# A state-space layer and a SwiGLU block on one NeuronCore: another order for the steps of a hand-scheduled kernel

## The chip, the core and the metric

The kernel runs on one core of a Trainium2 chip. A core has five engines with a queue of instructions each: TensorE (PE: matrix products and transposes, into PSUM), VectorE (DVE), ScalarE (ACT), GpSimd (POOL) and SyncE (SP, which issues the transfers here). Each engine takes its own queue strictly in order; engines wait for one another through semaphores. The metric is the device time of one execution in microseconds, as the median of several.

## The reference

A Mamba-2 layer (4 batches, 8 heads, 768 positions, head width 32, state width 16, chunks of 32 positions), whose output becomes 3072 tokens of 256 features, followed by an RMS norm and a SwiGLU block:

```python
log_a = np.log(np.clip(a, 1e-06, 1.0))
for c in range(nc):
    cum = np.cumsum(la, axis=-1)
    L = np.exp(cum[:, :, :, None] - cum[:, :, None, :]) * causal
    CB = np.einsum('bhin,bhjn->bhij', Cc, Bc)
    y_intra = np.einsum('bhij,bhjd->bhid', CB * L, xc)
    y_inter = np.einsum('bhin,bhnd->bhid', Cc, state) * np.exp(cum)[:, :, :, None]
    y[:, :, sl] = y_intra + y_inter
    Bx = np.einsum('bhjn,bhjd->bhjnd', Bc, xc) * decay_from_j[:, :, :, None, None]
    state = decay_full[:, :, None, None] * state + np.sum(Bx, axis=2)
x = y.transpose(0, 2, 1, 3).reshape(B * S, H * D)          # 3072 x 256
xn = x / np.sqrt(np.mean(x * x, -1, keepdims=True) + 1e-06) * rms_g
g = xn @ w_gate                                            # 256 x 1536
silu = g * (1.0 / (1.0 + np.exp(-g)))
return (silu * (xn @ w_val) @ w_out).astype(np.float32)    # 1536 x 256
```

The weights come in as 64-bit floating-point words.

## The kernel before

The work is one function. The 3072 tokens are six blocks of 512; a block is two pairs, a pair two stretches of 128 positions. For each pair the state-space part runs: load B, C (`bc`) and x (`x`), transpose them on PE (`turn`, with the copies out of PSUM `T`, `Tt`, `Td`), build the decays (`mask` L443 and `sums` L457/L464 on PE, `exp` on ACT, or by rows through DRAM with `row`, `rowout`, `rowe`, `tok`, `spread`, `sub`, `ex`), products of C and B (`g` L572/L579), their multiplication by the decays on DVE (`L`, `L1`; L618, L612), states (`A` L644 on PE, `S` L658 to L668 on DVE) and outputs (`y`, L685 to L716). Then follow squares, transposes and norm of a block (`sq`, `yt`, `ms`, `rs`, `rb`, `xn`).

The SwiGLU block of the first two pairs of block 0 is done plainly (`early`, `norm`; `gate.2` to `gate.5` at L845, `silu`, `hid` L878). Everything after uses a scheme with seven products in place of eight: sums of the weights (`cw` L900) and of the activations (`tx` L908), products `P.k.j` (L931), a copy of one of them by ACT (`take` L937), a sum on DVE (`C` L943), `silu` on ACT and the multiplication of both halves (`hid`, L956). The second projection of block 0 is plain (`o`); the later blocks use a similar scheme of larger order (`two`, `u`, `O` L1052, totals `w` L1083), and `put` stores the result.

Weights are loaded in twenty pieces (`fetch.k`, L148 to L160: pieces 0 to 3 of 256 KB, the rest of 512 KB) and turned from 64-bit words into 32-bit numbers: three activations for the exponent (`pow.k`, L184 to L190), two DVE operations for the mantissa (`man.k`, L209 and L212), and one that multiplies them (`wt.k`, L218).

The order of all this is written out. Under `tc.manual_schedule()` nothing is rearranged: a string `order` of 1649 steps is read from left to right, and each step emits its instructions on the queues of the engines that it uses. A step reads `block:kind.numbers/slots*fillers`; slots are the PSUM pairs (0, 1, 2) that it takes, and `c*2` puts two warm-up products ahead of the step `c`. The `p` at the end of a kind (`cwp`, `txp`, `hidp`, `up`, `twop`, `subp`) puts the same elementwise operation on POOL instead of DVE. So moving a step in the string moves all of its instructions in their engines' queues, its transfers on SP's queue included. There are eight semaphores for transfers; each transfer waits for the landing of the one eight before it. The loop that reads the string:

```python
for step in order.split():
    step, _, slots = step.partition("/")
    blk, _, step = step.partition(":")
    ...
    if blk == "0":
        first_kinds[kind](*numbers)
    else:
        kinds[kind](int(blk), *numbers)
```

Of the kernel before, what the change touches and what calls it, by code (L numbers as in the profile page):

```python
# [20 lines left out]
def kernel(  # L21
# [35 lines left out]
    P = 128  # L57
# [6 lines left out]
    T = NB * S  # L64
# [1154 lines left out]
    def of_chunk(n, fn):  # L1219
# [32 lines left out]
        0:mask.0.0/0 0:whole 0:hmask 0:tmask 0:part 0:gcol 0:part2 1:exps 0:after2 0:mask.0.1/1  # L1252
        0:fetch.3 0:aT 0:sel 0:la0 0:turn.0.1 0:T.0.1 0:Tt.0.1.1 0:log4.4.2 0:mask.1.1/2 0:Tt.0.0.1
        0:fetch.4 0:log4.0.4 0:r.0 0:parts.0 0:log 0:d 0:dx 0:log4.6.2 0:turn.0.0 0:Tt.0.0.0
        0:Tt.0.1.0 0:sums.0.1 0:exp.0.1 0:fetch.2 0:middles 0:T.0.0 0:sums.1.1 0:scale.0 0:sums.0.0
        0:kinks 0:scale.1 0:bc.2 0:turn.1.1 0:exp.0.0 0:T.1.1 0:Tt.1.1.1 0:Tt.1.0.1 0:man.0 0:c*2
        0:fetch.5 0:man.1 0:g.0.1/1 0:L.0.1 0:cx 0:exp.1.1 0:g.0.0/0 0:never16 0:last.1 0:Tl.1
        0:turn.1.0 0:Tt.1.0.0 0:fetch.8 0:L.0.0 0:T.1.0 0:Tt.1.1.0 0:mask.1.0/1 0:pow.0 0:A.0
        0:fetch.11 0:cc 0:S.0 0:A.1 0:sums.1.0 0:S.1 0:g.1.0/2 0:exp.1.0 0:L.1.0 0:pow.3 0:g.1.1/0
        0:eps 0:row.1 0:last.0 0:Tl.0 0:y.0/1 0:rowout.1 0:rowe.1 0:L.1.1 0:scale.2 0:fetch.7 0:wt.0  # L1260
        0:y.1/2 0:fetch.6 0:sq.0 0:pow.1 0:r.1 0:dT.2 0:turn.2 0:yt.0 0:x.2 0:man.3 0:wt.1 0:sq.1
        0:yt.1 0:pow.2 0:bc.3 0:parts.1 0:wt.3 0:T.2 0:man.2 0:wt.2 0:mask.3/1 0:man.4 0:early.0.0/0
        0:mask.2/2 0:man.5 0:ms.0 0:x.3 0:pow.4 0:rs.0 0:xn.0 0:sums.3 0:txp.0.0 0:tx.0.2 0:sums.2
        0:row.0 0:exp.3 0:Tt.2.0 0:Tt.2.1 0:fetch.9 0:Td.2 0:rowe.0 0:early.0.1 0:norm.0 0:pow.5
        0:exp.2 0:early.1.0/1 0:wt.5 0:early.1.1 0:silu.0 0:rowout.0 0:wt.4 0:fetch.10 0:man.6
        0:man.7 0:pow.7 0:norm.1 0:A.2 0:S.2 0:hid.0 0:gate.2/0 0:bc.5 0:table.0 0:pow.6 0:wt.7
        0:man.9 0:wt.6 0:gg.2/1 0:L1.2.3 0:L.2.0 0:silu.2 0:scale.3 0:man.8 0:pow.8 0:pow.9 0:hid.2
        0:gate.3/2 0:L1.2.2 0:wt.8 0:silu.3 0:hid.3 0:wt.9 0:pow.10 0:man.10 0:gate.4/1 0:y.2/2
        0:fetch.15 0:man.11 0:silu.4 0:wt.10 0:table.1 0:ydone.1 0:pow.11 0:ydone.0 0:S.3 0:sq.2
        0:scale.5 0:hid.4 0:yt.2 0:cw.3.0 0:cwp.3.1 0:gate.5/0 0:silu.5 0:wt.11 0:hid.5 0:cw.3.3  # L1270
        0:dT.3 0:turn.3 0:T.3 0:Tt.3.0 0:fetch.13 0:switch.1 0:Tt.3.1 0:Td.3 0:pow.13 0:man.13
        0:P.2.3 0:switch.0 0:P.2.4 0:P.1.3 0:fetch.12 0:cw.4.0 1:table 0:gg.3/2 0:take.1.3 0:cwp.4.1
        0:P.1.4 0:take.1.4 0:tx.0.1 0:cwp.3.2 0:P.6.3 0:L1.3.2 0:take.6.3 0:L.3.0 0:tok 0:L1.3.3
        1:dT.1 0:silu.1 0:cwp.4.2 0:C.11.3 0:P.6.4 0:take.6.4 0:P.7.3 0:C.11.4 0:wt.13 0:P.5.3
        0:tokout 0:take.7.3 0:fetch.14 0:pow.12 0:x.4 0:P.7.4 0:txp.0.3 0:P.4.3 0:man.14
        0:silug.11.4 0:C.22.3 0:silug.22.3 0:hidgp.22.3 0:bc.4 0:scale.4 0:man.12 0:x.5 0:P.3.3
        0:wt.12 0:silug.21.3 0:y.3/2 0:hidg.21.3 0:pow.14 0:P.1.5 0:C.12.3 0:P.2.5 1:S.0 1:S.1
        0:spread.10 0:spread.8 0:fetch.19 0:take.7.4 0:take.1.5 0:cwp.5.0 0:fetch.16 0:cwp.5.1
        0:spread.11 0:sq.3 0:P.5.4 0:fetch.17 0:C.22.4 0:P.6.5 0:hidgp.11.4 0:yt.3 0:wt.14
        0:take.6.5 0:cw.5.2 0:silug.12.3 0:P.4.4 0:ms.1 0:hidgp.12.3 0:C.11.5 0:silug.21.4 0:rs.1  # L1280
        1:spread.0 0:hidg.21.4 0:man.15 0:exps 0:hid.1 0:o.0/2 0:P.7.5 0:cw.1.0 0:cwp.4.3 0:P.3.4
        0:cw.1.1 0:C.12.4 0:pow.15 0:wt.15 0:cw.1.2 1:turn.0 1:T.0 0:silug.11.3 0:hidg.11.3
        0:silug.11.5 0:silug.12.4 0:hidg.12.4 0:take.7.5 0:rb.1 0:pow.16 0:P.5.5 0:o.1 0:o.2
        0:C.22.5 0:silug.22.4 0:man.16 0:P.4.5 0:silug.22.5 0:cw.1.3 0:cwp.5.3 0:cw.0.0 0:hidgp.11.5
        0:P.3.5 0:C.12.5 0:fetch.18 1:turn.1 0:silug.12.5 1:T.1 1:Tt.1.1 0:xn.1 0:silug.21.5 0:o.3
        0:cwp.0.2 0:hidg.21.5 1:P.1.0 1:take.1.0 0:txp.1.0 0:txp.1.2 1:P.2.0 0:tx.1.1 1:P.1.1
        0:ydone.3 0:wt.16 0:cwp.0.1 0:hidgp.22.4 1:P.6.0 1:P.2.1 1:bc.1 1:C.11.0 0:man.17 1:Tt.1.0
        1:take.1.1 1:silu.11.0 1:P.6.1 1:take.6.1 1:cwp.2.0 0:o.4 1:C.11.1 1:P.5.1 0:hidgp.12.5
        1:hid.11.0 0:hidgp.22.5 0:man.19 1:take.6.0 0:pow.19 0:wt.19 1:silu.11.1 1:P.7.1 1:take.7.1
        0:subp.10 0:txp.1.3 1:P.5.0 1:P.7.0 0:spread.9 1:P.4.1 1:C.22.1 1:P.3.1 1:Tt.0.0 1:silu.22.1  # L1290
        1:spread.3 1:hidp.22.1 1:Td.1 1:take.7.0 1:C.22.0 1:silu.21.1 1:P.4.0 0:pow.17 0:cw.0.3
        1:P.3.0 1:hid.21.1 0:man.18 1:silu.21.0 1:hid.11.1 1:C.12.0 0:ydone.2 1:spread.2 1:hid.21.0
        1:sub.0 1:cwp.2.2 1:P.1.2 0:sub.8 1:take.1.2 0:o.5 0:wt.17 1:C.12.1 1:sub.3 1:silu.12.0
        0:pow.18 1:hid.12.0 0:wt.18 1:two.2 1:cwp.2.1 1:P.6.2 1:Tt.0.1 1:P.1.3 1:take.1.3 1:take.6.2
        1:P.2.2 1:two.3 0:sub.11 1:P.2.3 1:P.7.2 1:silu.22.0 0:o.6 1:P.6.3 1:hid.22.0 0:o.7 1:x.0
        1:take.7.2 1:C.11.2 1:C.11.3 1:cw.2.3 1:P.5.2 2:dT.0 1:scale2.1 1:two.11 1:sub.2 1:ex.0
        0:sub.9 1:two.0 1:silu.11.2 1:P.4.2 1:take.6.3 0:ex.9 0:ex.8 1:two.1 1:twop.4 1:silu.11.3
        1:C.22.2 1:hid.11.3 1:P.7.3 1:take.7.3 1:silu.22.2 1:P.5.3 1:P.3.2 1:C.12.2 1:twop.6
        1:silu.12.1 1:hid.12.1 1:ex.3 1:C.22.3 0:o.8 1:silu.21.2 1:hid.21.2 1:P.4.3 1:bc.0
        1:silu.21.3 1:hid.21.3 1:scale2.0 0:o.9 1:hid.22.2 1:P.3.3 1:C.12.3 1:two.9 1:P.1.5  # L1300
        1:silu.22.3 1:take.1.5 1:P.1.4 1:take.1.4 0:o.10 0:o.11 1:hid.22.3 1:P.2.5 1:silu.12.3
        1:hidp.12.3 1:P.2.4 1:hid.11.2 1:P.6.4 1:C.11.5 1:spread.1 0:ex.10 0:ex.11 1:ex.2 1:dT.0
        1:Td.0 1:C.11.4 1:P.6.5 1:silu.11.5 0:put.0 0:put.3 0:put.1 0:put.2 1:g 1:L1.3 1:silu.11.4
        1:take.6.4 1:take.6.5 1:L 1:twop.8 1:L1.2 1:P.7.4 1:P.7.5 1:hid.11.5 1:P.5.4 1:take.7.4
        1:take.7.5 1:P.4.4 1:P.4.5 1:silu.12.2 1:two.5 1:C.22.4 1:y.0 1:silu.22.4 1:hid.11.4
        1:hidp.12.2 1:silu.21.5 1:hid.21.5 1:u.1 2:S.0 1:P.5.5 1:hid.22.4 1:silu.21.4 1:hid.21.4
        1:u.0 1:two.7 1:C.22.5 1:P.3.4 1:O.2.0 1:silu.22.5 1:C.12.4 1:silu.12.4 1:O.2.1 1:hid.22.5
        1:O.15.0 1:O.15.1 1:w.0 1:w.2 2:bc.1 1:x.1 1:u.2 1:y.1 2:S.1 1:P.3.5 1:C.12.5 1:O.3.0
        1:subp.1 1:O.3.1 1:sq 2:spread.2 1:yt 1:silu.12.5 1:O.0.0 1:O.0.1 1:hidp.12.5 1:O.6.0 1:up.9
        2:turn.0 1:u.3 1:ms 1:w.4 1:O.17.0 1:u.4 1:O.17.1 1:rs 1:w.5 1:w.10 1:O.6.1 1:O.16.0  # L1310
        1:O.16.1 1:w.1 1:u.5 1:O.4.0 1:rb 1:O.4.1 1:O.9.0 2:T.0 2:turn.1 1:u.6 1:O.9.1 1:w.6
        1:hidp.12.4 1:up.7 1:w.3 1:u.10 1:u.11 1:O.8.0 1:O.8.1 1:O.13.0 1:O.18.0 1:O.18.1 1:w.11
        1:O.13.1 1:O.11.0 1:w.12 1:w.8 2:dT.1 1:up.12 1:O.11.1 1:O.12.0 1:O.12.1 1:w.13 1:w.16 1:xn
        1:txp.0 1:txp.1 1:O.5.0 1:O.5.1 2:Tt.0.1 2:Tt.0.0 1:w.7 1:w.9 1:u.8 1:w.20 1:two.10 2:P.1.1
        2:take.1.1 2:P.1.0 1:O.7.0 1:O.7.1 1:up.13 1:w.14 1:w.17 1:w.15 2:take.1.0 2:P.6.1 1:w.18
        1:tx.2 2:P.6.0 1:u.14 1:O.1.0 2:take.6.1 1:O.1.1 1:up.15 1:O.14.0 1:O.14.1 1:O.19.0
        2:spread.0 1:w.19 1:O.19.1 2:spread.3 1:w.22 2:Td.0 1:w.24 2:T.1 2:Tt.1.1 1:O.10.0 2:Tt.1.0
        1:w.23 2:take.6.0 1:O.10.1 1:w.25 1:w.21 2:P.7.1 2:P.2.1 2:C.11.1 2:P.2.0 1:ex.1 2:P.7.0
        2:P.5.1 2:silu.11.1 2:take.7.0 2:C.11.0 2:Td.1 2:g 1:tx.3 2:sub.3 2:take.7.1 2:scale2.1
        2:P.4.0 2:silu.21.0 2:C.22.1 2:hid.11.1 2:silu.11.0 2:hid.11.0 2:hid.21.0 2:P.5.0 2:C.22.0  # L1320
        2:P.4.1 2:silu.21.1 2:subp.0 2:P.3.1 2:silu.22.1 2:x.0 2:L1.2 2:P.1.2 2:bc.0 2:scale2.0
        2:hid.21.1 2:hidp.22.1 2:take.1.2 2:C.12.1 2:silu.12.1 2:hidp.12.1 2:P.3.0 2:L 2:P.1.3
        2:take.1.3 2:P.6.2 2:take.6.2 2:P.2.3 2:C.12.0 2:L1.3 2:subp.2 2:C.11.3 2:y.0 2:silu.12.0
# [132 lines left out]
```

## Time and profile before

| what | us |
|---|---|
| median of 3 runs | 397.82 (397.78, 397.82, 398.51) |
| the profiled execution | 399.72 |
| its span, first to last instruction | 398.0 |
| mean granted clock of TensorE | 0.991 |
| first product of the scheme, L931 | starts at 55.19 |
| `mask.1.0`, the second pair's decays | starts at 15.77 |
| `r.1`, after the second pair's outputs | starts at 25.00 |

The profile is of one execution. "Busy" counts the time in which an engine runs an instruction; PE's counts the modelled ends of pipelined matmuls, so that a busy PE may still be waiting between them. The granted clock is the share of full speed at which TensorE was allowed to run. A timeline line gives the start, the length, engine, line, operation, output and input tiles with their shapes, and in brackets the idle time before it with what ended it.

### The profile page before, as it was taken

Reading aid. Unit: us, or ns where it says so; the run is one execution under the profiler, and the core shown is the slowest. Engines: PE = TensorE matmul, PEld = TensorE weight load, DVE = VectorE, ACT = ScalarE, POOL = GpSimd, SP = SyncE. Lnnn points to the kernel's source line nnn. Section 1 sums busy time; section 2 is a strip of 40 time slices with the busy share of each in tenths; the row PEclk is TensorE's granted clock in tenths of the full one; section 3 lists DMA queues with packets and bytes.
Section 4 is the critical chain, followed back from the end, with each engine's and each line's share of the span. In section 5 each row is a group of like instructions: output and inputs, shape, how many; then the busy total and the mean of one; then the engine's idle time right before and its main releaser. Section 6 shows DMA issues by size and latency. Waiting matters only on the chain.

```text
span 398.0 us, 9646 instructions
## 1 busy us (share of the span) xinstructions
PE 388.4 (98%) x3841; PEld 333.8 (84%) x3841; DVE 285.0 (72%) x617; ACT 236.2 (59%) x492; POOL 136.0 (34%) x157
## 2 busy tenths in 40 slices
PE   8799999999999999999999999999999999999996
PEld 4566468888887889988899988899988899988995
DVE  7789999998955877676586565677563577465684
ACT  3689989968898372556774534486256541455420
POOL 3110024366094345422276512144712042210121
PEclk9789999999999999999999999999999999999999
DMA  9898988275000516205013310210100001100001
GB/s 111 191 302 151 234 153 237 60 167 99 2 1 14 94 37 138 74 2 94 29 48 79 71 25 2 41 43 21 41 2 2 0 2 33 54 1 2 1 2 53
DMA packets 92469, 27.01 MB, mean 68 GB/s; under 512 B 77416, under 2 KB 86248, under 8 KB 92424
## 3 DMA queue, kind: packets, MB, share of 16 engines
q1 hardware_dynamic: 88264, 26.13, 29.9%
q10 hardware_dynamic: 4160, 0.26, 0.8%
q8 instruction: 30, 0.49, 0.5%
q14 instruction: 15, 0.12, 0.1%
HBM read 22.64 MB, written 3.74 MB: 66 GB/s over the span
## 4 chain that ended last, share of the span: by engine, by line
PE 79%; ACT 9%; DVE 4%; DMA 3%; issue 2%; SPq 1%; DVEq 0%; ACTq 0%
PE gate L931 27%; PE o L1052 22%; PE val L931 20%; PE o L963 4%; ACT e L190 3%; PE y L716 2%; DMA xr<-in_x_dram 2%; PE g L579 1%; DMA wr<-in_moe_w_gate_dram 1%; ACT L184 1%; ACT sq L190 1%; SPq L128 1%; DMA br<-in_B_dram 1%; ACT L L190 1%; PE tp L522 1%
## 5 line engine op out<-in xcount | busy, mean ns | idle before, releaser
L943 DVE TENSOR_TENSOR c<-val,p 128x512 f32<-128x512 f32 x99 | 67.2, 686 | 46.4 <-PE val L931 35.1
L937 ACT COPY p<-gate 128x512 f32<-128x512 f32 x99 | 56.9, 584 | 58.4 <-PE gate L931 57.4
L931 PE MATMUL gate<-tx,wgv 128*128 128x256 f32 x264 | 65.3, 380 | 0.0
L956 POOL TENSOR_TENSOR hid<-c 128x256 f32<-128x256 f32 x36 | 28.9, 805 | 106.1 <-ACT c L190 104.1
L190 ACT ACTIVATE c<-c 128x256 f32<-128x256 f32 x99 | 39.4, 414 | 33.6 <-DVE c L943 33.2
L931 PEld LDWEIGHTS gate<-tx,wgv 128*128 128x128 f32 x264 | 49.7, 190 | 7.1 <-issue 0.3
L1083 DVE TENSOR_TENSOR ob<-ob,o 128x128 f32<-128x128 f32 (+1 forms) x90 | 23.9, 297 | 24.1 <-PE o L1052 18.4
L956 DVE TENSOR_TENSOR hid<-c 128x256 f32<-128x256 f32 x63 | 28.3, 457 | 17.5 <-ACT c L190 15.6
L1052 PE MATMUL o<-two,hid 128*128 128x128 f32 x280 | 36.6, 276 | 0.2 <-ACT ob L190 0.2
L1052 PEld LDWEIGHTS o<-two,hid 128*128 128x128 f32 x280 | 34.1, 192 | 1.1 <-ACT ob L190 0.4
L931 PE MATMUL gate<-xn,wgv 128*128 128x256 f32 x132 | 33.6, 383 | 0.4 <-DVE hid L956 0.4
L931 PE MATMUL val<-tx,sw 128*128 128x256 f32 x132 | 33.8, 380 | 0.0
L931 PE MATMUL gate<-tx,sw 128*128 128x256 f32 x132 | 33.4, 382 | 0.0
L931 PE MATMUL val<-xn,sw 128*128 128x256 f32 x132 | 33.4, 381 | 0.0
L931 PE MATMUL val<-xn,wgv 128*128 128x256 f32 x132 | 32.8, 381 | 0.4 <-DVE hid L878 0.4
L492 POOL TENSOR_SCALAR_AFFINE_SELECT L<-L 64x512 f32<-64x512 f32 x32 | 24.9, 779 | 18.0 <-ACT L L190 16.6
L931 PEld LDWEIGHTS val<-xn,wgv 128*128 128x128 f32 x132 | 24.8, 190 | 4.0 <-DVE hid L878 0.7
L190 ACT ACTIVATE e<-e,kinks 128x512 f32<-128x512 int16 (+3 forms) x40 | 27.2, 679 | 1.3
L931 PEld LDWEIGHTS gate<-xn,wgv 128*128 128x128 f32 x132 | 24.3, 190 | 4.3 <-DVE hid L956 0.8
L931 PEld LDWEIGHTS val<-tx,sw 128*128 128x128 f32 x132 | 24.9, 190 | 3.4
L931 PEld LDWEIGHTS val<-xn,sw 128*128 128x128 f32 x132 | 24.6, 190 | 3.4 <-issue 0.2
L931 PEld LDWEIGHTS gate<-tx,sw 128*128 128x128 f32 x132 | 24.3, 190 | 3.4 <-issue 0.2
(203 smaller groups left out, 720.0 us busy)
## 6 DMA issues: line engine op xcount, KB each, us to landing
L<-rowd SPq DMA_DIRECT2D x32, 128.0 KB, 3.1
xr<-in_x_dram SPq DMA_DIRECT2D x24, 128.0 KB, 3.6
wr<-in_moe_w_out_dram SPq DMA_DIRECT2D x6, 512.0 KB, 6.9
out_dram<-ob SPq DMA_DIRECT2D x24, 128.0 KB, 1.8
wr<-in_moe_w_gate_dram SPq DMA_DIRECT2D x5, 512.0 KB
wr<-in_moe_w_val_dram SPq DMA_DIRECT2D x5, 512.0 KB, 5.7
br<-in_B_dram SPq DMA_DIRECT2D x22, 64.0 KB, 3.8
cr<-in_C_dram SPq DMA_DIRECT2D x22, 64.0 KB, 4.2
```

Of the source, the lines that this page charges most:

```text
L128: queue.dma_start(out=st[p]["x"][:, i], in_=x[b, :, sl, :].rearrange("h s n -> s h n"))
L184: nc.scalar.preload_act_table_set("natural_log_exp_and_others")
L190: nc.scalar.activation(**operands)
L492: nc.gpsimd.affine_select(out=L[r], in_=L[r], pattern=[[0, NH], [1, HC]], compare_op=ALU.is_ge, fill=0.0, base=0, channel_multiplier=-1)
L716: nc.tensor.matmul(out=y[2 * k + u][rows, (2 * n + i) * HC:(2 * n + i + 1) * HC], start=(k, u, rows.start) not in opened, stop=True, skip_ ...
L931: nc.tensor.matmul(out=dst[:, half[w]], lhsT=lhsT, rhs=rhs, start=(k in (1, 2, 5) and w == 0), stop=True, skip_group_check=True)
L937: nc.scalar.copy(out=t, in_=Xs[j])
L943: nc.vector.tensor_tensor(out=t, in0=Zs[j], in1=a, op=ALU.add)
L956: engine.tensor_tensor(out=hid[:, 2 * j + c // 10 - 1, c % 10 - 1], in0=u, in1=src[:, half[1]], op=ALU.mult)
L963: nc.tensor.matmul(out=o, lhsT=hid[:, f, k // 2, (k % 2) * P:(k % 2 + 1) * P], rhs=wo[:, f], start=opens, stop=(f == NF - 1), skip_group_c ...
L1052: nc.tensor.matmul(out=Os[blk, b][:, place * P:(place + 1) * P], lhsT=hidden_or_sum(u)[:, g], rhs=rhs, start=(blk, b) not in opened, stop= ...
L1083: nc.vector.tensor_tensor(out=o, in0=o, in1=src, op=ALU.add if what[0] == "+" else ALU.subtract)
```

## The change

One string is replaced: `order`. Its first 25 steps and its last 3 are the same; the 1621 between stand in another order. The steps are the same but for some that change their engine between DVE and POOL (`cw` and `cwp`, `tx` and `txp`, `hid` and `hidp`, `u` and `up`, `two` and `twop`, `sub` and `subp`): DVE has 445 elementwise operations of two tensors instead of 459, POOL 123 instead of 109. 2016 matmuls, 299 activations, 26 table loads and 189 transfers stay.

Named by what comes first in each queue: `man.0`, `man.1` and `pow.0` stand behind both halves `L.0.1`, `L.0.0` instead of ahead of them; `aT` is ahead of `mask.0.1`; the two filler products come ahead of `turn.0.0`; `cc`, `A.0` and `S.0` come ahead of `g.0.1`; the weights' pieces are fetched in another order (11, for one, behind `rowout.0`, where it stood behind 8); `turn.2`, `turn.3` and `tok` come between the plain products of block 0 instead of behind them; the gates run 2, 3, 5, 4 instead of 2, 3, 4, 5. The beginning of both:

```diff
-        0:mask.0.0/0 0:whole 0:hmask 0:tmask 0:part 0:gcol 0:part2 1:exps 0:after2 0:mask.0.1/1
-        0:fetch.3 0:aT 0:sel 0:la0 0:turn.0.1 0:T.0.1 0:Tt.0.1.1 0:log4.4.2 0:mask.1.1/2 0:Tt.0.0.1
-        0:fetch.4 0:log4.0.4 0:r.0 0:parts.0 0:log 0:d 0:dx 0:log4.6.2 0:turn.0.0 0:Tt.0.0.0
-        0:Tt.0.1.0 0:sums.0.1 0:exp.0.1 0:fetch.2 0:middles 0:T.0.0 0:sums.1.1 0:scale.0 0:sums.0.0
-        0:kinks 0:scale.1 0:bc.2 0:turn.1.1 0:exp.0.0 0:T.1.1 0:Tt.1.1.1 0:Tt.1.0.1 0:man.0 0:c*2
-        0:fetch.5 0:man.1 0:g.0.1/1 0:L.0.1 0:cx 0:exp.1.1 0:g.0.0/0 0:never16 0:last.1 0:Tl.1
-        0:turn.1.0 0:Tt.1.0.0 0:fetch.8 0:L.0.0 0:T.1.0 0:Tt.1.1.0 0:mask.1.0/1 0:pow.0 0:A.0
-        0:fetch.11 0:cc 0:S.0 0:A.1 0:sums.1.0 0:S.1 0:g.1.0/2 0:exp.1.0 0:L.1.0 0:pow.3 0:g.1.1/0
-        0:eps 0:row.1 0:last.0 0:Tl.0 0:y.0/1 0:rowout.1 0:rowe.1 0:L.1.1 0:scale.2 0:fetch.7 0:wt.0
-        0:y.1/2 0:fetch.6 0:sq.0 0:pow.1 0:r.1 0:dT.2 0:turn.2 0:yt.0 0:x.2 0:man.3 0:wt.1 0:sq.1
...
+        0:mask.0.0/0 0:whole 0:never16 0:hmask 0:tmask 0:fetch.2 0:part 0:eps 0:fetch.4 0:aT
+        0:after2 0:part2 0:mask.0.1/1 0:turn.0.1 0:la0 0:log4.4.2 0:T.0.1 0:Tt.0.0.1 0:mask.1.1/2
+        0:log4.0.4 0:log4.6.2 0:Tt.0.1.1 0:r.0 0:kinks 0:parts.0 0:log 0:d 0:middles 0:c*2 0:sel
+        0:dx 0:turn.0.0 0:scale.0 0:Tt.0.1.0 0:cx 0:sums.0.1 0:exp.0.1 0:Tt.0.0.0 0:fetch.3 0:gcol
+        1:exps 0:bc.2 0:sums.1.1 0:T.0.0 0:fetch.5 0:sums.0.0 0:exp.0.0 0:scale.1 0:cc 0:turn.1.1
+        0:T.1.1 0:A.0 0:S.0 0:g.0.1/1 0:L.0.1 0:g.0.0/0 0:last.1 0:Tt.1.1.1 0:fetch.8 0:Tt.1.0.1
+        0:exp.1.1 0:Tl.1 0:turn.1.0 0:T.1.0 0:Tt.1.1.0 0:Tt.1.0.0 0:bc.3 0:L.0.0 0:fetch.7 0:man.0
+        0:pow.0 0:man.1 0:mask.1.0/1 0:sums.1.0 0:g.1.1/0 0:g.1.0/2 0:L.1.1 0:exp.1.0 0:L.1.0
+        0:last.0 0:Tl.0 0:A.1 0:y.0/1 0:S.1 0:y.1/2 0:pow.1 0:sq.0 0:yt.0 0:wt.0 0:r.1 0:man.2
+        0:row.1 0:pow.4 0:wt.1 0:rowout.1 0:parts.1 0:sq.1 0:fetch.6 0:pow.2 0:wt.2 0:early.0.0/0
...
```

The steps around the first products of the scheme, before:

```diff
-        0:fetch.15 0:man.11 0:silu.4 0:wt.10 0:table.1 0:ydone.1 0:pow.11 0:ydone.0 0:S.3 0:sq.2
-        0:scale.5 0:hid.4 0:yt.2 0:cw.3.0 0:cwp.3.1 0:gate.5/0 0:silu.5 0:wt.11 0:hid.5 0:cw.3.3
-        0:dT.3 0:turn.3 0:T.3 0:Tt.3.0 0:fetch.13 0:switch.1 0:Tt.3.1 0:Td.3 0:pow.13 0:man.13
-        0:P.2.3 0:switch.0 0:P.2.4 0:P.1.3 0:fetch.12 0:cw.4.0 1:table 0:gg.3/2 0:take.1.3 0:cwp.4.1
...
```

and after:

```diff
+        0:fetch.10 0:rowe.0 0:rowout.0 0:exp.2 0:xn.0 0:early.0.1 0:early.1.0/1 0:txp.0.0 0:norm.0
+        0:silu.0 0:turn.2 0:man.7 0:hid.0 0:man.6 0:tok 0:ydone.1 0:tokout 0:early.1.1 0:gate.2/0
+        0:norm.1 0:pow.6 0:fetch.11 0:T.2 0:Tt.2.1 0:Tt.2.0 0:txp.0.2 0:ydone.0 0:wt.6 0:cwp.1.0
+        0:dT.2 0:man.11 0:turn.3 0:txp.0.1 0:Td.2 0:gate.3/2 0:pow.7 0:wt.7 0:dT.3 0:T.3 0:Tt.3.0
+        0:x.2 0:Tt.3.1 0:Td.3 0:silu.2 0:hid.2 0:gg.2/1 0:man.8 0:cw.1.1 0:L1.2.3 0:L.2.0 0:pow.11
+        0:wt.11 0:fetch.9 0:silu.3 0:man.10 0:pow.8 0:L1.2.2 0:gate.5/0 0:hid.3 0:pow.10 0:x.3
+        0:wt.8 0:A.2 0:S.2 0:silu.5 0:hid.5 0:cwp.1.2 0:tx.0.3 0:pow.9 0:man.9 0:wt.9 0:cwp.3.0
+        0:table.1 0:gate.4/1 0:silu.4 0:hid.4 0:pow.13 0:wt.10 0:y.2/2 0:S.3 0:cwp.3.1 0:cw.3.3
+        0:yt.2 0:cw.0.0 0:cwp.3.2 0:switch.1 0:P.2.3 0:switch.0 0:P.1.3 0:take.1.3 0:C.11.3 0:P.2.4
...
```

## The prediction

> **What bounds the kernel now.** I read the busy totals first, then PE's waits, then windows by stage, then the timeline where the windows show a hole.
>
> ```profile
> PE 388.4 (98%) x3841; PEld 333.8 (84%) x3841; DVE 285.0 (72%) x617; ACT 236.2 (59%) x492; POOL 136.0 (34%) x157
> PE e L443 <- DVE L L618: 2.6, 1, 2.6
> PE val L931 <- DVE hid L878: 0.4, 1, 0.4
> PE o L1052 <- DVE ob L1083: 0.4, 1, 0.4
> ```
>
> PE is busy for 98% of the span, and one wait stands out: `mask.1.0` (L443) is held 2.6 us, with DVE's `L` (L618) named. The windows tell whether "busy" means "the bound". Columns: window, length, then busy time and count of PE, PEld, DVE, ACT, POOL, then granted clock, DMA share, GB/s.
>
> ```profile
> 16.00:17.00 1.00, 1.00 (x14) 0.28 (x16) 0.97 (x2) 0.00 (x0) 0.00 (x0) 0.50 0.38 53
> 21.00:22.00 1.00, 1.00 (x8) 0.67 (x7) 0.58 (x4) 0.32 (x1) 0.00 (x0) 0.50 1.00 383
> 25.00:55.00 30.00, 29.10 (x344) 17.09 (x340) 29.14 (x65) 28.63 (x50) 2.43 (x3) 1.00 0.91 207
> 55.20:394.00 338.80, 337.72 (x3248) 302.19 (x3249) 235.47 (x488) 194.19 (x414) 127.93 (x136) 1.00 0.21 47
> ```
>
> Three stages. Up to 25 us latencies chain across engines, and the granted clock is 0.50 in part of it (by finer windows 1.00 from 5.0, 0.50 from 15.26 to 22.08, 1.00 from there). From 25 to 55 us DVE (29.14 of 30 us) and ACT (28.63) are both full, and PE's 29.10 are matmuls waiting for them. From 55.2 us PE is the bound: 337.72 of 338.80 us. So an earlier start of that last stage is worth its full amount, and an edit inside it only what PE loses there. The hole in the first stage:
>
> ```profile
> 12.58 1.06 POOL L421 TENSOR_TENSOR early<-early,hmask 128x416 f32<-128x416 f32 x1 [3.87 <-ACT early L190]
> 12.62 1.30 DVE L212 SCALAR_TENSOR_TENSOR m<-wr,m 128x256 f32<-128x256 uint32 x1
> 13.85 0.28 DVE L209 TENSOR_SCALAR m<-wr 128x256 int32<-128x256 int32 x1
> 14.16 0.43 DVE L212 SCALAR_TENSOR_TENSOR m<-wr,m 128x256 f32<-128x256 uint32 x1
> 14.50 1.22 DVE L618 TENSOR_TENSOR L<-g,L 128x1024 f32<-128x1024 f32 x1
> 15.77 1.01 PE L443 MATMUL e<-whole,ident 128*128 128x512 bf16 x2 [2.59 <-DVE L L618]
> ```
>
> DVE converts weight pieces 0 and 1 (`man.0`, `man.1`) from 12.29 to 14.50, and only then takes `L.0.1`, whose end frees the PSUM pair that `mask.1.0` writes. The first is stretched to 1.30 us beside a POOL multiplication; the second takes 0.43. The stage ends here:
>
> ```profile
> 54.46 0.67 DVE L878 TENSOR_TENSOR hid<-u,gate 128x512 f32<-128x512 f32 x1
> 55.19 1.99 PE L931 MATMUL val<-xn,wgv 128*128 128x256 f32 x8 [0.45 <-DVE hid L878]
> ```
>
> **The change part by part.** The string's first 25 and last 3 steps stay; all between are in another order, to the end of block 5, not only to about the 250th. Counts of matmuls, activations and transfers are equal; 14 elementwise operations go from DVE to POOL. Summed by row medians, DVE's work falls from 272.5 to 264.9 us, POOL's rises from 129.9 to 143.7, PE stays at 377.2, ACT at 235.0. No operation is new, so every cost below is a row's duration; only contention and waits need bounds.
>
> *Startup.* Up to `r.0` (6.19) and `parts.0` (ends 8.77) PE and DVE get the same work. I then walked the new queues with the durations of before's timeline. ACT: `exp.0.1` (1.0 us) 9.9 to 10.9, `exp.0.0` to 11.8, transposes' copies to 12.7, `exp.1.1` to 13.7, four copies to 14.9, `pow.0` (1.69) to 16.55, `exp.1.0` to 17.55, against 19.83. DVE: `cc` 0.58 to 11.5, `S.0` 0.83 to 12.3, `L.0.1` 1.22 to 13.5 (before 15.72), `L.0.0` to 14.7, only now `man.0` and `man.1` (1.4) to 16.1, `L.1.1` to 17.3, and `L.1.0` from 17.6 to 18.8; before, the later of these two ended at 23.09. PE: `mask.1.0` at 13.6 instead of 15.77, `y.0` 17.6 to 18.9, `y.1` to 20.6, where `r.1` follows; before, `r.1` stood at 25.00. So PE is 4.4 us earlier there. What is late next is the first weights: `man.0` ends at 15.4 rather than 13.92, but nothing asks for their product before `gate.2` (37.08). I take the clock at 1.00 throughout: the new order leaves PE idle by 0.3 to 0.7 us at a time, before had 2.59 at once just ahead of the half rate.
>
> *The full engines.* That 4.4 us doesn't pass whole. ACT from the end of `exp.1.0` to the last gate's silu has 33.5 us of work, summed over the new order by rows, and about 0.5 of waits (before it idled 1.37 in the 30 us window): 17.55 + 34.0 = 51.55, then `hid.4` 0.69: 52.25. DVE from 18.8 has 31.3 of work and 1.2 of waits (30 − 29.14 in that window, rounded up): 51.3. They end together, so ACT's path counts, plus what POOL costs DVE. Five more POOL operations stand between `xn.0` and `hid.4` (`txp.0.1`, `txp.0.2`, `cwp.1.0`, `cwp.1.2`, `cwp.3.0`), 4.35 us of POOL time in all. Nearest rows: the stretched L212 lost 0.87 us to one POOL operation of 1.06; over the run, 38 DVE operations exceed their medians by 15.06 us against 157 POOL operations, 0.10 us for each. Five by 0.10 is 0.5; bounds 0 and 4.35. I take 0.5, as most rows pay nothing. `P.2.3` then starts at 52.8 instead of 55.19: 2.4 us.
>
> The Trainium skill, page "SBUF — State Buffer", section "SBUF: two separate sides", says that a VectorE operation with two SBUF inputs and a GpSimd operation reading SBUF exclude one another for whole instructions. That speaks against moving work to POOL; the row at 12.62 agrees (1.30 against 0.43 us), the run's mean of 0.10 us does not ask for the whole price. By the rule at its worst the sum would be 399.0, a rival below.
>
> *Transfers* (SP's queue). Weight pieces are issued in another order, and eight are in flight: each waits for the one eight before. The tight ones by before's landing times (a 512 KB piece 5.7 to 7 us): `fetch.11`, now behind `rowout.0` on SP, issued about 32, lands 37.5 to 39, wanted by `man.11` at 37.8 (0 to 1.2 us, taken as 0 since DVE's lag covers it); `fetch.12` issued about 50, lands 56 to 57, wanted at 56 behind four waiting POOL and DVE steps, with PE's products queued well ahead.
>
> *The PE stage.* `tok` (0.33 us of PE, at 60.50 before) now runs ahead of `P.2.3`, so 0.33 less lies behind it. Along blocks 1 to 5 I compared, step by step, when an operand's producer stands in its queue against when PE asks: the tightest margin is no smaller than before's (0.00 before, 0.22 after), and the end (`O.1.0`, `O.14.0`; 0.4 lost to L1083 before) has the same one. Changed loss 0; bounds −1.1 (all that PE idles there, 338.80 − 337.72) and +2, twice the present loss, since every step's neighbours are new.
>
> **Sum.** −2.4 − 0.33 = −2.7 us. The profiled execution took 399.72 us (span 398.0 and 1.72 around it), 1.90 above the median of 397.82: 397.0 for a profiled one, 395.1 for the median. A repeat of this kernel differs by up to 0.7 us (397.78 to 398.51), so 0.2%, 0.8 us, is the bound of "same".
>
> **The rivals.**
> - *The whole startup gain carries* (0.08). The 4.4 us of `r.1` survive if ACT's and DVE's sums overlap better than I summed. For: DVE ends its list 4.3 us earlier. Against: ACT gains only 2.3 (19.83 to 17.55). 397.82 − 4.4 − 0.33 = 393.1.
> - *The half-rate stretch comes back* (0.14). Steps of the clock lie on a grid of 3.41 us in the trace (15.26 to 22.08 is two). If sparse PE work between 9 and 16 us still draws two steps at half rate, 6.83 us hold 3.4 us of full-rate work, some of it hidden by ACT and DVE. If ACT and DVE fall back by 2.0 to 2.7 of it: 397.1 to 397.8, no change. For: PE is only 75 to 80% busy there in my walk. Against: the 2.59 hole is gone.
> - *POOL locks DVE* (0.25, the other side). Place: between `xn.0` and `hid.4`, where DVE has no slack (29.14 of 30). If each of the five POOL operations holds DVE for its length, it pays 4.35 instead of 0.5: 397.82 − 2.7 + 3.85 = 399.0. It decides from about 3.2 us paid (then the gain is nil), and more so if later moved operations do the same. For: the row at 12.62. Against: 0.10 a piece over the run.
> - *It doesn't do what it says*: named for the steps to about the 250th, it reorders nearly all, so that the gain at the start may be lost later. That is the +2 bound: 397.1.
>
> In a sentence by itself: the Trainium skill, "TensorE: Matmul & The Clock Gate", section "Part 1: The HAM clock gate (the "warmup" mystery)", has the rate decided in free-running windows of 3413 ns whose phase varies by run; the trace agrees in the two rates (0.50, 1.00) and the 6.83 us, and by it the second rival would hit some executions and not others.
>
> **How the numbers follow.** Forecast 395.1 (0.53), its own range 393.3 (PE bound −1.1 and no POOL cost) to 397.1 (+2). Gain whole 0.08, clock 0.14, lock 0.25. Faster holds the forecast and the first rival, 0.61; within 0.2% the clock, 0.14; slower the lock, 0.25. For 8 in 10 the range must reach the slower case with its spread: 392.8 to 399.6.
>
> **What would show it.** In the new profile: PE's 2.6 us wait at L443 gone; `L.0.1` over by about 13.5; granted clock 1.00 between 15 and 22 us; `r.1` near 20.6; the first L931 at 51.7 to 54; from there to the last matmul 338.5 us. It is wrong if the first L931 is not before 54, if the clock shows 0.50 after 15 us, or if the L931 stage is longer than 340 us; the lock shows as DVE rows of L212, L218 or L900 above 1 us beside `txp` and `cwp`.

## The result and the profile after

The changed kernel took 396.88 us in the median of 8 runs (395.88 to 398.12); the kernel before, run beside it, 398.12 (8 runs, 397.78 to 398.79). The ratio is 0.9968 with an interval of [0.9953, 0.9983]: faster by 1.24 us. The forecast was 2.7 us. The two profiled executions differ by 2.89 us (399.72 and 396.83): nearly the forecast, in part by luck, as will be seen. The document's question is why these two differences are not the same.

The profile after, in the views that the prediction read. The page's busy totals, then three of PE's waits (in all, times, longest):

```profile
PE 388.5 (98%) x3841; PEld 333.4 (84%) x3841; DVE 286.7 (73%) x603; ACT 235.2 (60%) x492; POOL 152.3 (39%) x171
```

```profile
PE o L1052 <- DVE ob L1083: 0.9, 2, 0.5
PE val L931 <- DVE hid L878: 0.3, 1, 0.3
PE e L443 <- DVE L L618: 0.2, 1, 0.2
```

The wait of L443 is down from 2.6 to 0.2 us. The windows of the changed kernel (length, then PE, PEld, DVE, ACT, POOL, granted clock, DMA share, GB/s):

```profile
15.00:16.00 1.00, 0.80 (x8) 0.20 (x8) 1.00 (x2) 1.00 (x6) 0.00 (x0) 1.00 1.36 220
25.00:55.00 30.00, 29.23 (x343) 17.45 (x342) 29.14 (x62) 29.09 (x51) 6.23 (x8) 1.00 0.90 207
52.80:392.00 339.20, 338.20 (x3252) 302.38 (x3251) 238.69 (x481) 191.80 (x415) 140.96 (x146) 1.00 0.22 50
```

The half rate is gone, DVE and ACT are still full up to 52 us, and PE still bounds the rest. The timeline at the two places of the prediction, first the second pair's decays, then the first product:

```profile
14.13 2.35 DVE L618 TENSOR_TENSOR L<-g,L 128x1024 f32<-128x1024 f32 x2
16.39 0.28 DVE L209 TENSOR_SCALAR m<-wr 128x256 int32<-128x256 int32 x1
```

```profile
15.40 0.59 PE L443 MATMUL e<-whole,ident 128*128 128x512 bf16 x2 [0.20 <-DVE L L618]
52.55 1.13 PE L931 MATMUL val<-xn,wgv 128*128 128x256 f32 x4 [0.27 <-DVE hid L878]
```

`L.0.1` and `L.0.0` run back to back (x2), the weights' conversion (L209) behind them, and the first product starts at 52.55, against a forecast of 52.8.

But `mask.1.0` (15.40) is hardly earlier than before (15.77). The trace's record of the granted clock tells why: its first entry, called the rise from here on, sets full rate at 9.56 us in this execution and at 5.02 in the one before. (Ahead of the first entry the window view prints 1.00, as nothing is recorded there; the rows show the slower rate: the L443 pair at 5.91 takes 1.06 us here, the same pair at 5.74 in the execution before 0.59.) The two profiles are not of one case.

### The profile page after: what moved, and what is told of

It is laid out like the page before. It is cut to its first block, busy times and chain, and to the rows that moved or that the text cites. A ratio compares the mean times of both kernels' runs of the same rounds, so it can differ in the third digit from the quotient of the medians.

```text
span 395.1 us, 9640 instructions
## 1 busy us (share of the span) xinstructions
PE 388.5 (98%) x3841; PEld 333.4 (84%) x3841; DVE 286.7 (73%) x603; ACT 235.2 (60%) x492; POOL 152.3 (39%) x171
## 4 chain that ended last, share of the span: by engine, by line
PE 85%; DVE 7%; ACT 3%; DMA 2%; issue 2%; DVEq 0%; ACTq 0%
PE gate L931 29%; PE val L931 21%; PE o L1052 21%; PE o L963 5%; PE y L716 3%; DMA wr<-in_moe_w_val_dram 1%; PE g L579 1%; DMA cr<-in_C_dram 1%; DVE wgv L218 1%; DVE L L618 1%; DVE m L212 1%; ACT e L190 1%; PE tp L522 1%; PE y L644 1%; DVE m L209 1%
## 5 line engine op out<-in xcount | busy, mean ns | idle before, releaser
L956 POOL TENSOR_TENSOR hid<-c 128x256 f32<-128x256 f32 x42 | 35.2, 847 | 91.1 <-ACT c L190 88.9
L931 PE MATMUL gate<-tx,wgv 128*128 128x256 f32 x264 | 66.1, 382 | 0.0
L931 PEld LDWEIGHTS gate<-tx,wgv 128*128 128x128 f32 x264 | 48.9, 190 | 7.4 <-issue 0.5
L931 PE MATMUL val<-tx,sw 128*128 128x256 f32 x132 | 33.8, 381 | 0.0
L931 PE MATMUL val<-xn,sw 128*128 128x256 f32 x132 | 33.7, 380 | 0.0
L931 PE MATMUL val<-xn,wgv 128*128 128x256 f32 x132 | 33.3, 380 | 0.3 <-DVE hid L878 0.3
L931 PE MATMUL gate<-tx,sw 128*128 128x256 f32 x132 | 33.4, 381 | 0.0
L931 PE MATMUL gate<-xn,wgv 128*128 128x256 f32 x132 | 33.1, 379 | 0.0
L492 POOL TENSOR_SCALAR_AFFINE_SELECT L<-L 64x512 f32<-64x512 f32 x32 | 23.0, 719 | 13.5 <-ACT L L190 12.1
L931 PEld LDWEIGHTS val<-xn,wgv 128*128 128x128 f32 x132 | 24.9, 190 | 3.7 <-DVE hid L878 0.4
L931 PEld LDWEIGHTS val<-tx,sw 128*128 128x128 f32 x132 | 24.8, 190 | 3.7 <-DVE c L943 0.3
L931 PEld LDWEIGHTS gate<-tx,sw 128*128 128x128 f32 x132 | 24.6, 190 | 3.4 <-issue 0.2
L931 PEld LDWEIGHTS gate<-xn,wgv 128*128 128x128 f32 x132 | 24.6, 190 | 3.2
L931 PEld LDWEIGHTS val<-xn,sw 128*128 128x128 f32 x132 | 24.5, 190 | 3.2 <-issue 0.2
```

The source lines that it names most:

```text
L492: nc.gpsimd.affine_select(out=L[r], in_=L[r], pattern=[[0, NH], [1, HC]], compare_op=ALU.is_ge, fill=0.0, base=0, channel_multiplier=-1)
L931: nc.tensor.matmul(out=dst[:, half[w]], lhsT=lhsT, rhs=rhs, start=(k in (1, 2, 5) and w == 0), stop=True, skip_group_check=True)
L956: engine.tensor_tensor(out=hid[:, 2 * j + c // 10 - 1, c % 10 - 1], in0=u, in1=src[:, half[1]], op=ALU.mult)
```

## The experiments

**More executions of both kernels.** Two theories. A: the execution that the prediction was made from is not typical. B: it is typical, and the new order loses 1.5 us behind 55 us. The edit: none.

> The kernel before, unchanged, to see more executions of it. Theory A (phase): the profiled execution that the prediction was made from, 399.72 us, is not typical; its 6.83 us at half rate come from where TensorE's clock windows fell in that execution, and most executions have none. Then most executions show a mean granted clock of 0.998 or more, a span near 396.4, and the profile's first L931 lies at 53 to 54 us. Theory B (the new order gives something back): all executions of the kernel before look like the profiled one, clock 0.991 and first L931 near 55.2, and the 1.5 us that are missing from the forecast gain are lost behind 55 us by the new order.

> The changed kernel, unchanged, in more executions. Theory A: first L931 at 52.3 to 53 in whatever execution, clock 0.999 or 1.0 in all, time 396.5 to 397.2. Theory B: the same start of L931, but executions that lose 1 us or more between there and the last product, which the profile shows as waits of PE behind 55 us of over 2 us in all (1.2 in the first profile).

Each execution comes with its mean granted clock. Two windows of 3.41 us at half rate make it 0.991, one makes it 0.996. The executions of the kernel before in three sets of runs, each on a chip of its own (the eight above came without a clock; the profiled ones of 399.72 and of `before_3` are not counted):

| mean clock | executions | mean us | range |
|---|---|---|---|
| 0.990 or 0.991 | 36 of 87 | 399.46 | 399.0 to 399.9 |
| 0.995 or 0.996 | 11 of 87 | 398.43 | 398.06 to 398.78 |
| 0.998 or more | 40 of 87 | 397.99 | 397.18 to 398.68 |

The changed kernel had 20 executions, none below 0.999, mean 396.72. So the half rate strikes some executions of the kernel before, and those with two such windows take 1.5 us longer; none of the eight beside which the change was measured reached 399.0. Against the half-rate group the gain is 399.46 − 396.72 = 2.74 us; against the group at 0.998 or more, called undisturbed here, 1.27, which is what was measured. A holds for that comparison. Its "most executions have none" does not hold everywhere: two windows are lost in 11 of 39 executions of one set, 4 of 13 of another, but 21 of 35 of the third, whose median is 399.39. That median is 2.67 us above the changed kernel's mean, near the forecast gain, though the changed kernel was not run beside that set. Why the sets differ no run shows. The profile that was expected at 53 to 54 for the first L931 came at 52.84. B falls: in the changed kernel's second profile L931 starts at 52.60 and the last product 339.14 us later, as in the first (339.19).

The profiles point to a cause of the half rate. Windows of 3.41 us laid on the grid of the clock's own steps, the kernel before in the execution of the prediction, then in `before_again`, where the clock rose at 9.21:

```profile
11.85:15.26 3.41, 1.33 (x18) 0.81 (x11) 2.90 (x5) 3.38 (x9) 1.06 (x1) 1.00 1.02 317
15.26:18.67 3.41, 2.90 (x50) 1.89 (x53) 3.29 (x9) 0.56 (x2) 0.00 (x0) 0.50 0.66 82
```

```profile
12.62:16.04 3.42, 2.50 (x52) 1.48 (x44) 3.32 (x7) 3.39 (x10) 1.26 (x1) 1.00 1.09 297
```

PE was busy for 1.33 of 3.41 us (39%) and the next window ran at 0.50; with 2.50 (73%) it stayed at 1.00. Why the same kernel fills the window differently shows in the rows of `before_again`:

```profile
12.57 0.42 DVE L212 SCALAR_TENSOR_TENSOR m<-wr,m 128x256 f32<-128x256 uint32 x1
```

```profile
13.44 1.26 POOL L421 TENSOR_TENSOR early<-early,hmask 128x416 f32<-128x416 f32 x1 [3.47 <-ACT early L190]
```

```profile
14.96 0.59 PE L443 MATMUL e<-whole,ident 128*128 128x512 bf16 x2 [0.92 <-DMA wr<-in_moe_w_gate_dram]
```

After a late rise PE's first products run longer at half rate, so PE and POOL reach this place later (POOL's L421 at 13.44 instead of 12.58, past the L212 of `man.0`, which takes 0.42 instead of 1.30), while DVE starts on the weight that it waits for at the same time (12.23, before 12.29). The hole is 0.92 instead of 2.59: PE's last product ahead of it starts 0.85 later (13.76, before 12.91), and L443 0.81 earlier. In the execution of the prediction the early rise let PE run ahead into the hole.

**Filler products in front of the hole.**

```diff
-        0:turn.1.0
+        0:turn.1.0*10
```

> The kernel before with ten filler products (1.1 us at full rate, results unused) ahead of turn.1.0, just in front of the 2.6 us hole; nothing else moved. Theory A (too little PE activity in one clock window makes the half rate): clock 0.99 in none or at most 1 in 10 of the executions, against 11 of 39; the slow group at 399.2 to 399.7 is gone, and the median falls to 397.6 to 398.2. Theory C (the half rate comes from something else, power or the transfers): still 0.99 in about 3 of 10, and the median is not below 398.1.

None of 12 executions below 0.999, beside 25 of 35 of the kernel before in the same set: theory A's cause stands (too little PE work in one clock window), C falls. The time is 398.75 (ratio 0.9993 [0.9978, 1.0008]), above the expected 397.6 to 398.2: the fillers push `mask.1.0` to 16.03 in the profile, and that profile was the slowest of the twelve (400.0), with a stop in front of the first product:

```profile
53.72 0.67 DVE L878 TENSOR_TENSOR hid<-u,gate 128x512 f32<-128x512 f32 x1
```

```profile
55.65 1.89 PE L931 MATMUL val<-xn,wgv 128*128 128x256 f32 x8 [1.63 <-DVE wgv L218]
```

The row names the L218 that ends at 55.34, but in the kernel before the same product starts (55.19) ahead of that L218 (55.40). `hid.4`, for which it waits there, is over at 54.39 here, and 1.26 us later the product starts. What held it in between no row shows, so this stays open. The other eleven have a median of 398.65, still above the range: filling the hole removes the half rate, yet the time stays above the undisturbed 397.99.

**`man.0` and `man.1` alone.**

```diff
-        0:man.0 0:c*2 0:fetch.5 0:man.1 0:g.0.1/1 0:L.0.1
+        0:c*2 0:fetch.5 0:g.0.1/1 0:L.0.1
...
-        0:L.0.0
+        0:L.0.0 0:man.0 0:man.1
```

> The kernel before with man.0 and man.1 alone put behind both L.0.1 and L.0.0. It takes away the 2.6 us hole ahead of mask.1.0. Theory A: the hole alone makes the half rate, so no execution has a clock below 0.998, and the time is that of the kernel before without half rate or up to 0.6 us less (396.9 to 398.1), since DVE and ACT are full behind it. Theory B: 396.5 or less, nearly the whole gain that was forecast.

No half rate in 12 executions, as A expects, but 398.77 us (ratio 1.001 [0.9996, 1.0023]), above its range. Its profile shows what took the hole's place:

```profile
PE r_ps L1127 <- DVE A L658: 1.0, 1, 1.0
PE y L694 <- DVE L L618: 0.5, 1, 0.5
```

The conversions now stand ahead of the states (`S`, L658), for which PE waits at `row.1`; the second wait stands in `before_again` too. The first L931 comes at 54.66, after a rise at 10.27; this profile is the slowest of the twelve (399.21).

**Eight early steps as in the new order.**

```diff
-        0:r.0 0:parts.0 0:log 0:d 0:dx ... 0:turn.1.1 0:exp.0.0 0:T.1.1 ... 0:man.0 0:c*2
+        0:r.0 0:parts.0 0:log 0:d 0:sel 0:c*2 0:dx ... 0:cx ... 0:turn.1.1 0:cc 0:exp.0.0 0:T.1.1 0:A.0 0:S.0
...
-        0:L.0.0
+        0:L.0.0 0:man.0 0:man.1
```

> The kernel before with eight steps moved: c, sel, cx, cc, A.0 and S.0 to the places that they have in the new order, man.0 and man.1 behind L.0.0; all else as before, the transfers too. e1_man moved man.0 and man.1 alone and got a new wait of 1.0 us at row.1 for DVE's states. If the start's few steps suffice, no execution shows the half rate, y.0 stands at 17 to 18.7 and the time is 396.6 to 397.4, near the changed kernel. If the stage from 22 to 52 us takes the start's gain back unless it is reordered too (as e2_head suggests), the half rate is gone as well, but the time is that of the undisturbed executions of the kernel before, 397.7 to 398.6.

The half rate is gone (10 of 10, with a rise at 4.33 in the profile), and the time is 398.54 (range 397.68 to 399.63; ratio 1.0006 [0.9988, 1.0024]): the second answer. The start alone is worth nothing beyond the undisturbed executions of the kernel before. The ten fall into two groups, five at 397.7 to 398.1 and five at 399.0 to 399.6, all at a mean clock of 1.0. So something besides the half rate moves the time by as much; the time of the rise, which the mean clock does not show, is a candidate (the profile with its early rise is in the faster group), but no profile shows the slower one.

**Cut and joined orders.** The new order up to `y.1` with the old behind it (`e2_head`), and the reverse (`e3_tail`):

> The steps of the new order up to y.1 (the first 107), then all others in the order before. It tells where the gain arises. Both theories: y.1 over at about 22 us as in the changed kernel. Theory A: the gain of the start carries in part, first L931 at 52.5 to 53.5, time 396.4 to 397.4. Theory B, where the rest of the new order loses what the start wins: 395.4 or less, below the changed kernel.

> The steps of the order before up to y.1, then all others in the new order: the counterpart of e2_head. If the gain lies behind the start (the new order of weights, transfers and gates between 22 and 52 us), the time is 397.0 or less where no clock window is lost, and the half rate still hits about 3 executions in 10, since the hole ahead of mask.1.0 is still there. If head and rest only fit together, the time is above that of the kernel before (398.5 or more), as e2_head's was (400.62).

Both lose: 400.62 (1.0063 [1.0043, 1.0084]), above both ranges, and 399.97 (1.0027 [1.0013, 1.004]). Waits of PE in `e2_head`, then in `e3_tail`:

```profile
PE A_ps L644 <- ACT e L190: 1.3, 1, 1.3
...
PE A_ps L644 <- DMA xr<-in_x_dram: 0.7, 1, 0.7
```

```profile
PE e L443 <- DVE L L618: 2.4, 1, 2.4
```

In the first, `y.1` starts early (18.72), and then PE waits for the x of the third pair, fetched too late for this start, and for ACT; the first L931 comes at 55.84 in a profile without any half rate. Two of its six executions do show it (0.991 and 0.996), although its order leaves no hole at L443 (0.2 in the profile); where it fell in them no profile shows. In the second the hole is back, and with it the half rate in 7 of 10. Head and rest fit only together.

**The new order up to the first product, then the old.**

> The new order up to P.2.3, the first product, then the order before. The forecast gave 2.4 of 2.7 us to this part and 0.33 to tok, which is in it too: by the forecast's own split it should come out like the changed kernel, 396.4 to 397.2, with no half rate. If the new order of the long stage behind gives anything of its own, this one is slower than the changed kernel by more than 0.5 us; if it takes something, faster.

The median is 397.71 us (0.9974 [0.996, 0.9987] on a chip where the kernel before often lost two windows; its median was 399.39): 0.99 above the changed kernel's mean of 396.72. No half rate in 10. The first L931 comes at 51.98 (rise at 7.94), so the start is all there. The loss is one wait of PE in the seam:

```profile
PE gate L931 <- POOL sw L900: 1.0, 1, 1.0
```

The old rest wants a weight sum (at 58.50) earlier than POOL has it, which itself waits 1.76 us for a sum of DVE's. So the new order behind the first product is needed, though it earns little by itself.

**The five POOL operations back on DVE.**

```diff
-        0:txp.0.2 ... 0:cwp.1.0 ... 0:txp.0.1 ... 0:cwp.1.2 ... 0:cwp.3.0
+        0:tx.0.2 ... 0:cw.1.0 ... 0:tx.0.1 ... 0:cw.1.2 ... 0:cw.3.0
```

> The changed kernel with the five operations txp.0.1, txp.0.2, cwp.1.0, cwp.1.2 and cwp.3.0 on DVE instead of POOL. If POOL locks DVE for whole operations (the rival of the prediction), the five cost DVE as much on POOL as on DVE or more, and the first L931 comes at 52.6 or earlier: time 396.7 or less. If the lock is seldom paid (0.1 us for each), DVE gets 2.4 us of work in its full stretch and the first L931 comes 1 to 2.4 us later: 397.5 to 399.

The median is 397.75 us, 1.03 above the changed kernel's mean, and the wait in front of the first product grows from 0.3 to 1.1:

```profile
PE val L931 <- DVE hid L878: 1.1, 1, 1.1
```

The first L931 comes at 53.00 after a rise at 4.9 (51.53 in the changed kernel after a rise at 4.64). So POOL takes work off a full DVE here and costs it less than it saves. Counted as in the prediction, the rows of DVE that exceed their medians do so by 0.7 us between 25 and 52.5 us in the changed kernel. Over the whole run the price is higher: the excess rises from 15.1 to 22.6 us, 0.54 us for each of the 14 operations that POOL has more, and DVE is busy for 286.7 us instead of 285.0 although it has 14 operations fewer. That all of this comes from POOL is not shown. Behind the first product PE sets the time, so this costs nothing there. The Trainium skill, page "SBUF — State Buffer", section "SBUF: two separate sides", has a VectorE operation with two SBUF inputs and a GpSimd operation that reads SBUF exclude one another for whole instructions; the trace agrees that single rows stretch, but in the full stretch the five operations of 4.35 us are not paid in full.

**Three more profiles.**

> One more profile of the changed kernel, in the hope of a first clock rise near 5 us. With an early rise r.1 should stand near 20.5 (as in e6_five, rise at 4.9), no half rate follows, and the first L931 comes at 51.8 to 52.6; with a late rise r.1 near 22.1 and the first L931 near 52.6 as in the two profiles so far.

> As after_3: a fourth execution of the changed kernel. The first L931 does not move by more than 0.8 us whatever the rise, if ACT and DVE set it.

> A third profile of the kernel before. With a rise before 6 us: the hole ahead of mask.1.0 is over 2 us and the half rate follows within 16 us, first L931 near 55. With a rise of 7 us or later: a hole of at most 1.3 us, no half rate or one window of 3.4 us, first L931 at 52.8 to 54.

All profiled executions of both kernels, starts in us; the last column but one is from the start of the first L931 to the start of the last product:

| execution | rise | hole at L443 | half rate | `r.1` | first L931 | to the last product | time |
|---|---|---|---|---|---|---|---|
| before, of the prediction | 5.02 | 2.59 | 15.26 to 22.08 | 25.00 | 55.19 | 339.41 | 399.72 |
| before_again | 9.21 | 0.92 | none | 22.24 | 52.84 | 339.51 | 397.48 |
| before_3 | 9.70 | 0.9 | none | 22.33 | 53.48 | 339.42 | 398.03 |
| after_4 | 4.64 | 0.21 | none | 20.25 | 51.53 | 339.13 | 395.75 |
| after | 9.56 | 0.20 | none | 22.04 | 52.55 | 339.19 | 396.83 |
| after_again | 9.98 | 0.2 | none | 22.18 | 52.60 | 339.14 | 396.86 |
| after_3 | 10.30 | 0.2 | none | 22.28 | 52.71 | 339.17 | 396.96 |

`before_3` came as expected for a late rise. `after_4` is the early rise that was hoped for; its first L931 is 1.02 to 1.18 earlier than the others', more than the 0.8 expected there, and slightly ahead of the 51.8 expected in `after_3`: what ACT and DVE have to do starts earlier too (`exp.1.0` is over at 16.69, in the first profile at 18.48). Its rows at the two places:

```profile
13.61 0.59 PE L443 MATMUL e<-whole,ident 128*128 128x512 bf16 x2 [0.21 <-DVE L L618]
```

```profile
51.53 1.13 PE L931 MATMUL val<-xn,wgv 128*128 128x256 f32 x4 [0.27 <-DVE hid L878]
```

Like with like, then: after an early rise the change is worth 399.72 − 395.75 = 3.97 us (one execution each), after a late one 397.76 (mean of two) − 396.88 (mean of three) = 0.87. The changed kernel's 20 executions lie between 395.75 and 398.12 without any half rate; what makes the slowest of them no profile shows.

## Why the prediction was wrong

The step that failed is the last of the sum, "397.0 for a profiled one, 395.1 for the median". It carried a gain worked out from one execution over to a median of others, though it had noted that the execution stood 1.90 us above that median. It stood there because of the half rate and the long hole, which were the very things that the gain removed; the two profiled executions near that median (397.48 and 398.03) had a hole of 0.9 us and no half rate, so 1.5 of the 2.7 us were not there to be saved. Both numbers that showed it were in hand before: the highest of the three times was 398.51, and a mean clock of 0.991 stood beside 399.72.

By the terms:
- *Startup, with an early rise.* Right to a tenth at its beginning and to 0.4 at its end: in `after_4` `L.0.1` is over at 13.56 (13.5 forecast), `L.1.0` at 18.43 (18.8), `r.1` stands at 20.25 (20.6). `exp.1.0` is over at 16.69 (17.55), the last silu at 50.39 (51.55): the forecast put ACT's copies and `pow.0` 0.9 us too late, and this is most of the 1.3 us by which the first L931 (51.53) beats 52.8. That the changed kernel's first profile met 52.8 (52.55) came from a late rise, 1.1 us later, that made up for it.
- *"I take the clock at 1.00 throughout"*: right for the changed kernel behind the rise, in 20 of 20 executions. That the rise can come as late as 9.56 to 10.30 us, as in three of its four profiles, it did not foresee. The rival put the half rate into the changed kernel; it belonged to the old one, in some executions only.
- *The whole 4.4 us does not pass*: right in kind. After an early rise `r.1` gains 4.75 and L931 3.66; after a late one, 0.1 and 0.5.
- *POOL's cost, 0.5 us*: 0.7 by rows, and moving the five back costs 1.0. The rival that gave 399.0 falls. The price of 0.10 us for each operation was a mean over all; the 14 added ones come with 0.54 each over the run, where it did not matter.
- *Two sums*: the lower end of its own range, 395.1 less 1.1 and less 0.5, is 393.5 and not 393.3; and DVE's waits of 1.2 are more than 30 − 29.14 = 0.86. Neither changes the forecast, for which ACT's path counted.
- *`tok` and the PE stage, −0.33 and 0*: from the first L931 to the last product the kernel before took 339.45 us (mean of three), the changed one 339.16 (mean of four): −0.29. No transfer of the named ones shows up as a wait of PE.
- *It doesn't do what it says* falls too: the reordered steps behind the first product lose nothing, and `e4_to55` shows that they are needed.

The Trainium skill, page "TensorE: Matmul & The Clock Gate", section "Part 1: The HAM clock gate (the "warmup" mystery)", has the rate decided in free-running windows of 3413 ns, from run to run at another phase. The traces agree: two rates, steps that lie multiples of 3.41 us apart, and rises from 4.33 to 10.30 us over the profiles here. The prediction gave that rule to the changed kernel alone; given to both, it says that the profile of before is one draw of several. The phase alone does not account for the rises: they spread over 6 us, more than one window.

## What to carry to other kernels

Before a gain read from one profile is subtracted from a median, ask whether that execution is one of the median's kind: its time against the range of the others, its mean clock against 1. What is special about a slow execution is not saved in the rest. And an order that is tight across five engines doesn't come apart: its head, its rest and its two most visible moves each gave nothing or a loss alone.

## What the runs showed of the hardware

A hole of 2.4 to 2.6 us in PE's work was enough for the half rate when 2.1 to 2.3 us of it lay in one clock window. PE was busy for 39% of that window in the execution of the prediction and for 33% in `e3_tail`; both were followed by 0.50. With 62% in `e7_early` and 52% later in `e5_fill` the clock stayed at 1.00. One line each, in the order `e3_tail`, `e7_early`, `e5_fill`:

```profile
12.10:15.52 3.42, 1.14 (x14) 0.63 (x7) 3.28 (x6) 3.35 (x10) 1.21 (x1) 1.00 0.89 259
11.16:14.57 3.41, 2.11 (x36) 1.51 (x37) 3.34 (x11) 3.32 (x10) 1.72 (x4) 1.00 1.06 330
53.86:57.27 3.41, 1.78 (x10) 1.62 (x9) 3.35 (x8) 2.75 (x6) 1.11 (x1) 1.00 0.90 91
```

For the way back up, PE's busy share alone does not decide. In the execution of the prediction a window of 85% at half rate (2.90 of 3.41 us) was followed by a second one; in `e3_tail` 96% (3.28 of 3.41) was enough. But in `after_3` both windows from 3.48 to 10.30 us are busy throughout, and the first of them brought no rise; in the execution of the prediction one such window, from 1.61 to 5.02, was followed by it. What else decides is not shown. Executions with two windows at half rate took 1.5 us of 398 longer, those with one 0.4. In the three profiles of the kernel before, the rise went with the case: at 5.02 a hole of 2.59 us and the half rate, at 9.21 and 9.70 a hole of 0.9 and none. Over all profiles here it came between 4.33 and 10.30 us, though PE's first product starts at 1.11 us in each.
